# Sliding-window attention with a gated MLP on one core: the order of all steps and the engines of casts and copies, written anew

## The chip, the core and the metric

The kernel runs on one NeuronCore of a Trainium2 chip. TensorE (PE; its weight loads are listed as PEld) multiplies matrices into PSUM, VectorE (DVE), ScalarE (ACT) and GpSimd (POOL) work on elements, SyncE (SP) issues most of the DMAs. The metric is the device time in microseconds; smaller is better. The inputs are q, k and v (float32, 8 batches, 8 heads, 576 positions, 64 values each) and four weights; the output is (8, 576, 512) in float32. Inside, matrices are multiplied in float16.

## What is computed

```python
scores = scale * np.matmul(q, k.transpose(0, 1, 3, 2))
mask = (rel >= 0) & (rel < 64)                 # rel = query position - key position
attn = softmax of scores where mask holds
x = attn @ v, heads side by side               # (8, 576, 512)
h = np.maximum(x @ w_in, 0.0)                  # 1024 columns: u first, then v
u, v = h[..., :512], h[..., 512:]
v_n = (v - mean) / sqrt(var + 1e-6)            # over the 512 columns
v_s = einsum('ts,bsd->btd', w_spatial, v_n) + b_spatial
out = (u * v_s) @ w_out
```

## The kernel before

Each of the 8 batches goes through the same steps. The positions are cut into tiles (indices 0 to 3, and a short one, 4), heads into pairs. A string, ORDER, names 1195 steps one after the other; a loop at its end (L653) splits each word at its dots and calls the function for it. Each engine takes its own instructions in the order in which they come, so this string is the program of all five queues at once; a tile scheduler adds the semaphores but moves nothing. The words, with batch b first:

- `l.b.q.s`, `l.b.k.s` (L301 to L310): loads of q and k by SP. For b below 4 a head pair of 256 KB, and for s = 4 a piece on 64 partitions; from b = 4 on, one head of 144 KB on 32 partitions. `lv.b.n` (L317 to L323): loads of v.
- `c` (L331 to L337): casts of q and k to float16; `cv` (L343, L346): casts of v; `sh` (L351 to L360): a copy of v shifted by 64 partitions. Their last letter is the engine: A ScalarE, D VectorE, P GpSimd.
- `T` (L378, L381): transposes of q and k by PE into PSUM, and `to` (L388, L391), their copies back to SBUF, for b below 4; from b = 4 on `R` (L369) transposes on VectorE.
- `S` (L410, L421): scores by PE; `E` (L453 to L460): the exponential by ScalarE; `M` (L469): the mask as a minimum, by VectorE; `P` (L486, L496): row sums and attention times v by PE; `n1`, `n2` (L502, L509): one over the sum, as logarithm and exponential, by ScalarE; `x` (L517): the product by VectorE, which ends the attention of a tile.
- `wl.half.r` and `wc.half.r` (L251, L254): load and cast of a block of w_in; half 1 is the v half. The loaded blocks share five buffers with the outputs. `wsp` and `wout`: loads by GpSimd's queue; `W`, `wo` (L271, L276): the spatial weight transposed.
- `V.b.j.r0.r1` (L531): the v half of x @ w_in, matmuls r0 to r1 of four; `Q.b` (L543, L546): the short tile of V together with that of O of the batch before; `vo` (L554, L556): relu; `bs` (L562): statistics; `rs` (L569): their root; `ln` (L580): the normalized values.
- `U`, `ru` (L589 to L602): the u half and its relu; `G` (L612), `g` (L619): the spatial matmul and the gate; `O` (L626), `oc` (L633), `st` (L639): output, its eviction and its store by SP.
- `H.n` (L644): n matmuls on a tile of zeros, which keep PE busy in the start.

PSUM buffers: scores and attention outputs share two large ones (tag `att`), so that the third S waits for the first x; all else shares four of one bank each (tag `mm`). An SP load waits for its buffer, and everything behind it on SP's queue waits with it. All loads of SP use eight semaphores in turn, so a ninth waits for the first to land.

Of the kernel before, what the change touches and what calls it, by code (L numbers as in the profile page):

```python
# [14 lines left out]
S = 576  # L15
# [5 lines left out]
keep scratch table l.0.k.0 H.6 id mask l.0.q.1 maskr l.0.q.0 lv.0.1 ones.0 l.0.q.2 ones.1 lv.0.0 H.2  # L21
lv.0.2 c.0.k.0.A l.0.k.1 H.2 l.0.k.2 lv.0.3 T.0.k.0 H.3 c.0.q.0.A l.0.k.3 c.0.q.1.A lv.0.8 T.0.q.0
to.0.q.0.A T.0.q.1 c.0.q.2.D l.0.q.4 to.0.q.1.A small cv.0.0.P to.0.k.0.A sh.0.0.1.D H.4 l.0.k.4
sh.0.0.0.D wl.1.0 c.0.k.1.A S.0.0 E.0.0 T.0.k.1 c.0.k.2.P H.3 lv.0.5 to.0.k.1.D lv.0.4 M.0.0 S.0.1
l.0.q.3 T.0.k.2 cv.0.1.D E.0.1 H.2 wl.1.1 T.0.q.2 sh.0.1.1.P wl.0.1 P.0.0 to.0.k.2.A M.0.1 lv.0.6
n1.0.0 H.3 c.0.k.4.P lv.1.2 n2.0.0 c.0.q.4.P sh.0.1.0.A P.0.1 lv.0.7 c.0.k.3.P n1.0.1 wl.1.3 T.0.k.4
to.0.q.2.A T.0.q.4 l.1.q.0 cv.0.2.D to.0.k.4.A x.0.0 T.0.k.3 n2.0.1 sh.0.2.1.P l.1.k.0 c.0.q.3.A
to.0.q.4.D wc.1.0.P S.0.2 x.0.1 H.4 wl.1.2 cv.0.4.P E.0.2 to.0.k.3.D sh.0.2.0.P wl.0.3 T.0.q.3
wc.1.1.A S.0.4 to.0.q.3.D l.1.q.1 V.0.3.0.1 E.0.4 M.0.2 wl.0.2 S.0.3 wc.0.1.A V.0.2.0.1 E.0.3 lv.1.0
cv.0.3.D P.0.2 V.0.3.1.2 wc.1.3.D wl.0.0 n1.0.2 V.0.0.0.1 sh.0.3.0.D V.0.0.1.2 M.0.3 sh.0.3.1.A  # L30
lv.1.1 n2.0.2 sh.0.4.0.D P.0.3 M.0.4 l.1.k.1 n1.0.3 x.0.2 wc.1.2.P l.1.q.2 P.0.4 n2.0.3 wsp
V.0.3.2.3 n1.0.4 x.0.3 lv.1.3 V.0.0.2.3 V.0.2.1.2 n2.0.4 wc.0.3.A lv.1.4 x.0.4 V.0.3.3.4 V.0.2.2.3
vo.0.3.A V.0.0.3.4 l.1.k.3 wc.0.2.D V.0.2.3.4 c.1.q.0.P vo.0.0.A V.0.1.0.1 l.1.q.3 V.0.1.1.2
vo.0.2.A c.1.k.0.P V.0.1.2.3 wc.0.0.P bs.0.2 Q.0 V.0.1.3.4 T.1.k.0 cv.1.0.P vo.0.1.A U.0.0 vo.0.4.D
c.1.q.1.P to.1.k.0.A bs.0.0 T.1.q.0 U.0.4 c.1.k.1.P to.1.q.0.A bs.0.4 U.0.3 sh.1.0.1.P ru.0.4 lv.1.5
ru.0.0 bs.0.1 S.1.0 ru.0.3 T.1.q.1 U.0.2 E.1.0 bs.0.3 c.1.q.2.P T.1.k.1 sh.1.0.0.A M.1.0 U.0.1
l.1.k.2 to.1.q.1.A l.1.q.4 to.1.k.1.D ru.0.2 W.1 rs.0 l.1.k.4 ru.0.1 W.3 ln.0.4 ln.0.3 W.0 wo.3.A
ln.0.1 P.1.0 wo.1.D cv.1.1.A lv.1.6 ln.0.2 W.4 wo.0.A ln.0.0 l.2.k.0 c.1.k.3.P S.1.1 wo.4.D n1.1.0
W.2 wout lv.1.7 T.1.k.3 wo.2.A T.1.q.2 G.0.1 l.2.k.4 cv.1.2.P to.1.k.3.A l.2.q.0 n2.1.0 sh.1.1.1.P
c.1.k.2.D G.0.0 lv.1.8 to.1.q.2.A c.1.q.3.P sh.1.1.0.A l.2.q.1 g.0.1 E.1.1 T.1.k.2 G.0.4 sh.1.2.1.P  # L40
g.0.0 G.0.2 to.1.k.2.A c.1.k.4.P x.1.0 c.1.q.4.A M.1.1 sh.1.2.0.A S.1.2 g.0.4 T.1.k.4 E.1.2 T.1.q.4
g.0.2 P.1.1 l.2.k.1 T.1.q.3 to.1.k.4.A G.0.3 M.1.2 n1.1.1 lv.2.2 c.2.k.0.D n2.1.1 l.2.k.2 P.1.2
to.1.q.4.D cv.1.3.P g.0.3 n1.1.2 O.0.0 lv.2.1 sh.1.3.1.P x.1.1 n2.1.2 O.0.2 lv.2.0 to.1.q.3.A x.1.2
c.2.q.0.P S.1.3 oc.0.2.D S.1.4 cv.1.4.P E.1.3 T.2.k.0 oc.0.0.D lv.2.3 O.0.3 sh.1.4.0.P to.2.k.0.A
M.1.3 lv.2.5 T.2.q.0 c.2.q.1.P O.0.1 sh.1.3.0.A to.2.q.0.D lv.2.4 E.1.4 P.1.3 oc.0.3.D lv.3.3 n1.1.3
V.1.1.0.2 M.1.4 lv.3.2 V.1.3.0.2 n2.1.3 oc.0.1.D l.2.q.4 V.1.3.2.3 c.2.k.2.A P.1.4 x.1.3 l.2.q.2
cv.2.0.P S.2.0 n1.1.4 V.1.1.2.3 l.2.k.3 n2.1.4 V.1.1.3.4 cv.2.1.P V.1.3.3.4 lv.2.7 x.1.4 vo.1.1.A
U.1.1 c.2.k.1.P vo.1.3.D l.2.q.3 E.2.0 sh.2.1.1.P V.1.2.0.2 sh.2.0.0.D lv.2.6 T.2.q.1 cv.2.2.P
sh.2.0.1.A V.1.2.2.3 bs.1.1 lv.3.6 V.1.2.3.4 ru.1.1 V.1.0.0.2 vo.1.2.A V.1.0.2.3 M.2.0 V.1.0.3.4
c.2.q.4.P T.2.k.1 c.2.k.4.A lv.3.0 P.2.0 to.2.k.1.D vo.1.0.A sh.2.1.0.P st.0.0 Q.1 to.2.q.1.A bs.1.2  # L50
n1.2.0 c.2.k.3.P lv.3.1 bs.1.3 S.2.1 oc.0.4.A sh.2.2.1.P l.4.q.1 U.1.4 vo.1.4.A bs.1.0 lv.3.7
T.2.k.2 cv.3.1.P U.1.3 n2.2.0 l.3.k.0 c.2.q.2.P to.2.k.2.D ru.1.4 E.2.1 U.1.2 cv.2.3.P x.2.0 lv.3.5
c.2.q.3.P bs.1.4 T.2.q.2 ru.1.3 U.1.0 sh.2.2.0.P l.3.q.1 to.2.q.2.A M.2.1 l.3.k.4 rs.1 T.2.k.3
ru.1.2 S.2.2 lv.2.8 ln.1.1 P.2.1 ln.1.0 ru.1.0 l.3.q.0 ln.1.2 n1.2.1 T.2.q.4 ln.1.4 l.3.k.1 T.2.q.3
ln.1.3 G.1.3 to.2.k.3.A l.3.k.3 sh.2.3.1.D to.2.q.3.A to.2.q.4.A G.1.0 st.0.2 E.2.2 st.0.3 n2.2.1
G.1.1 M.2.2 lv.3.4 x.2.1 l.3.q.3 S.2.3 g.1.0 P.2.2 E.2.3 cv.2.4.P l.3.q.2 g.1.3 G.1.4 sh.2.3.0.P
g.1.1 n1.2.2 st.0.1 G.1.2 M.2.3 n2.2.2 l.4.q.2 x.2.2 T.2.k.4 P.2.3 to.2.k.4.A l.3.k.2 c.3.k.3.P
g.1.2 n1.2.3 S.2.4 c.3.k.0.P O.1.1 lv.4.4 g.1.4 E.2.4 c.3.k.4.P l.4.q.7 n2.2.3 O.1.0 sh.2.4.0.P
oc.1.1.D cv.3.0.A l.3.q.4 M.2.4 O.1.2 oc.1.0.A sh.3.0.1.P x.2.3 cv.3.3.A V.2.2.0.4 l.4.k.1 c.3.k.1.P
c.3.q.1.A sh.3.1.0.P oc.1.2.A l.4.k.3 P.2.4 vo.2.2.D O.1.3 n1.2.4 st.0.4 sh.3.0.0.P cv.3.2.D n2.2.4  # L60
sh.3.1.1.P c.3.q.0.A V.2.1.0.4 x.2.4 sh.3.3.1.A oc.1.3.D lv.4.1 c.3.q.2.P V.2.0.0.4 vo.2.1.A bs.2.2
l.4.q.4 c.3.k.2.P T.3.q.0 st.1.3 sh.3.2.1.P vo.2.0.D T.3.k.0 to.3.q.0.A V.2.3.0.4 l.4.k.0 c.3.q.3.P
bs.2.1 to.3.k.0.A T.3.k.2 cv.4.4.P vo.2.3.A T.3.k.1 bs.2.0 S.3.0 sh.3.2.0.P to.3.k.2.A T.3.q.1
lv.4.2 T.3.q.2 to.3.k.1.A c.3.q.4.P to.3.q.1.D l.4.k.2 Q.2 E.3.0 sh.3.3.0.P bs.2.3 S.3.1 vo.2.4.A
M.3.0 T.3.k.3 cv.4.1.P to.3.q.2.A U.2.2 bs.2.4 E.3.1 sh.4.4.0.P P.3.0 to.3.k.3.D ru.2.2 lv.4.0 S.3.2
oc.1.4.D rs.2 lv.3.8 U.2.0 n1.3.0 l.4.q.5 ln.2.2 M.3.1 U.2.1 n2.3.0 E.3.2 l.4.q.6 x.3.0 T.3.q.3
U.2.3 l.4.q.3 ru.2.0 l.4.q.0 M.3.2 to.3.q.3.A P.3.1 st.1.1 ln.2.3 ru.2.1 P.3.2 ln.2.0 lv.4.3 ln.2.1
ru.2.3 T.3.q.4 st.1.2 T.3.k.4 ln.2.4 n1.3.2 G.2.2 to.3.k.4.D st.1.0 to.3.q.4.A l.4.k.5 n1.3.1 G.2.0
# [617 lines left out]
```

## Time and profile before

| what | value |
|---|---|
| median of 5 runs | 213.35 us (212.08 to 216.94) |
| the profiled execution's own time | 215.84 us |
| its span, first to last instruction | 214.1 us |
| mean granted PE clock | 0.99 |
| DMA traffic | 41.47 MB, 194 GB/s over the span |
| short-tile pv matmuls (Q) start at | 28.8, 59.1, 83.2, 106.9, 129.0, 152.3, 173.4 and 194.2 us |

How to read the profile: busy times are those of one execution; "x" is a count of instructions. A row of a group gives line, engine, operation, out<-in and shape, then busy time and the mean of one. In the slices, each digit is the busy share in tenths of 5.35 us. The Q starts cut the run into stages, one per batch: while the gated MLP of one batch runs on PE, the attention of the next is worked in between.

### The profile page before, as it was taken

How to read it: one execution, taken by the hardware profiler on the slowest of the kernel's cores; microseconds unless marked ns; L12 is line 12 of the kernel's file. 1: busy time of each engine (PE TensorE's matmuls, PEld its weight loads, DVE VectorE, ACT ScalarE, POOL GpSimd, SP SyncE). 2: the span in 40 equal slices, each digit the busy share in tenths (PEclk: the TensorE clock that was granted, in tenths of full speed). 3: DMA queues.
4: the chain of work that ended last, by engine and by line, in shares of the span. 5: the costliest groups of instructions: out<-in, count | busy, mean ns of one | idle time of the engine just before them, and what ended most of it. 6: DMA issues, size and time to landing. Idle time of an engine off the chain costs nothing.

```text
span 214.1 us, 6690 instructions
## 1 busy us (share of the span) xinstructions
PE 200.0 (93%) x2726; PEld 106.8 (50%) x2726; DVE 166.8 (78%) x328; ACT 172.4 (81%) x320; POOL 73.7 (34%) x109
## 2 busy tenths in 40 slices
PE   7677899899999999999999998999999999999992
PEld 2344445555555546655555554465554645454450
DVE  2245898799796879979999889888987798778650
ACT  7777979988999699978877799989998798665512
POOL 2126583545761678035300744042303450000000
PEclk9997999999999999999999999999999999999999
DMA  5999999999989999994799799997999423000415
GB/s 179 283 213 298 327 239 240 199 205 227 245 227 228 343 189 239 199 302 62 204 242 184 160 221 234 241 172 214 259 208 174 130 87 126 0 3 21 186 55 182
DMA packets 77742, 41.47 MB, mean 194 GB/s; under 512 B 44368, under 2 KB 72080, under 8 KB 77712
## 3 DMA queue, kind: packets, MB, share of 16 engines
q1 hardware_dynamic: 76544, 39.86, 83.3%
q0 software_dynamic: 1168, 1.19, 3.3%
q8 instruction: 21, 0.34, 0.8%
q14 instruction: 9, 0.07, 0.1%
HBM read 32.79 MB, written 9.44 MB: 197 GB/s over the span
## 4 chain that ended last, share of the span: by engine, by line
PE 58%; ACT 20%; DVE 7%; SPq 4%; issue 4%; DMA 3%; POOL 2%; ACTq 0%; DVEq 0%; POOLq 0%
PE ps L612 17%; PE po L626 9%; PE pu L589 8%; PE pv L531 6%; ACT e L453 4%; PE oz L486 4%; PE sc L421 3%; DMA vf<-in_v_dram 3%; PE oz L496 3%; ACT ln L502 2%; ACT ru L602 2%; ACT zi L509 2%; PE pv L543 2%; ACT vs L556 2%; SPq L301 2%
## 5 line engine op out<-in xcount | busy, mean ns | idle before, releaser
L612 PE MATMUL ps<-wspT,vn 128*128 128x512 f16 (+1 forms) x256 | 38.7, 286 | 0.8 <-DVE wspT L276 0.8
L453 ACT ACTIVATE e<-sc 128x1024 f16<-128x1024 f32 x32 | 32.6, 1026 | 4.8 <-PE sc L410 3.9
L531 PE MATMUL pv<-win,x 128*128 128x512 f16 x128 | 32.2, 382 | 0.9 <-DVE x L517 0.7
L589 PE MATMUL pu<-x,win 128*128 128x512 f16 x128 | 31.4, 379 | 0.0
L619 DVE TENSOR_TENSOR g<-ps,ru 128x512 f16<-128x512 f32 (+1 forms) x40 | 24.6, 629 | 8.2 <-PE ps L612 8.2
L626 PE MATMUL po<-wout,g 128*128 128x512 f16 x128 | 30.8, 380 | 0.0
L517 DVE TENSOR_TENSOR x<-oz,zi 128x512 f16<-128x512 f32 (+1 forms) x40 | 25.1, 630 | 6.3 <-ACT zi L509 5.8
L469 DVE TENSOR_TENSOR e<-e,mask 128x1024 f16<-128x1024 f16 x32 | 26.3, 821 | 4.2 <-ACT e L453 3.9
L502 ACT ACTIVATE ln<-oz 128x512 f32<-128x512 f32 (+1 forms) x40 | 22.0, 554 | 9.1 <-PE oz L496 8.9
L562 DVE BATCH_NORM_STATS2 st<-vs 128x6 f32<-128x512 f16 (+1 forms) x40 | 26.8, 669 | 0.5 <-ACT vs L556 0.4
L612 PEld LDWEIGHTS <-vn 128*128 128x128 f16 x256 | 17.0, 97 | 15.4 <-DVE vn L580 2.1
L509 ACT ACTIVATE zi<-ln 128x512 f32<-128x512 f32 (+1 forms) x40 | 23.4, 594 | 0.7
L602 ACT ACTIVATE ru<-pu 128x512 f32<-128x512 f32 (+1 forms) x40 | 21.1, 553 | 1.4 <-PE pu L594 0.7
L556 ACT ACTIVATE vs<-pv 128x512 f16<-128x512 f32 (+1 forms) x29 | 16.7, 598 | 5.4 <-PE pv L531 3.7
L360 POOL COPY vs<-vn 64x512 f16<-64x512 f16 (+1 forms) x16 | 12.6, 789 | 18.7 <-ACT vn L346 15.0
L633 ACT COPY ob<-po 128x512 f32<-128x512 f32 (+1 forms) x23 | 13.1, 585 | 7.2 <-PE po L626 6.8
L531 PEld LDWEIGHTS <-x 128*128 128x128 f16 x128 | 11.3, 98 | 14.5 <-DVE x L517 2.5
L626 PEld LDWEIGHTS <-g 128*128 128x128 f16 x128 | 11.3, 97 | 12.1 <-DVE g L619 1.1
L589 PEld LDWEIGHTS <-win 128*128 128x128 f16 x128 | 11.6, 98 | 11.5
L612 PE MATMUL ps<-wspT,vlast 65*128 65x512 f16 (+1 forms) x64 | 17.3, 288 | 0.0
L346 POOL CAST vn<-vf 64x512 f16<-64x512 f32 (+1 forms) x12 | 8.1, 683 | 21.7 <-DMA vf<-in_v_dram 21.5
L496 PEld LDWEIGHTS <-vn 128*64 128x64 f16 x320 | 13.6, 112 | 3.2
(130 smaller groups left out, 368.4 us busy)
## 6 DMA issues: line engine op xcount, KB each, us to landing
out_dram<-ob SPq DMA_DIRECT2D x32, 256.0 KB, 3.8
vf<-in_v_dram SPq DMA_DIRECT2D x40, 128.0 KB, 5.8
fq<-in_q_dram SPq DMA_DIRECT2D x32, 144.0 KB, 5.1
fk<-in_k_dram SPq DMA_DIRECT2D x32, 144.0 KB, 5.5
fk<-in_k_dram SPq DMA_DIRECT2D x16, 256.0 KB, 6.2
fq<-in_q_dram SPq DMA_DIRECT2D x16, 256.0 KB, 5.8
vf<-in_v_dram SPq DMA_DIRECT2D x16, 256.0 KB, 5.9
wf<-in_moe_w_in_dram SPq DMA_DIRECT2D x8, 256.0 KB, 5.0
```

The lines of the kernel that those rows point to most:

```text
L453: nc.scalar.activation(e2[:, :, :], sc[0][:, :, :], AF.Exp, bias=0.0, scale=0.125)
L469: nc.vector.tensor_tensor(e2[:, :, :], e2[:, :, :], m, ALU.min)
L502: nc.scalar.activation(lnz[:, 0:n], OZ[b, s][:, 1, 0:n], AF.Ln)
L509: nc.scalar.activation(zinv[:, 0:n], lnz[:, 0:n], AF.Exp, bias=0.0, scale=-1.0)
L517: nc.vector.tensor_tensor(x[:, 0:n], oz[:, 0, 0:n], zinv[:, 0:n], ALU.mult)
L531: nc.tensor.matmul(PV[b, j][0:jn, :], xcol(b, r, j), w_in_sb[:, r, 512:1024], start=(r == 0), stop=(r == 3))
L562: nc.vector.bn_stats(st6[0:jn, 0:6], VSB[b, j][0:jn, :])
L589: nc.tensor.matmul(pu[:, :], w_in_sb[:, r, 128 * m:128 * m + 128], X[b, r][:, :], start=(r == 0), stop=(r == 3))
L602: nc.scalar.activation(RU[b, m][:, 0:n], pu[:, 0:n], AF.Relu)
L612: nc.tensor.matmul(o, VN[b, kk][0:kn, 128 * mm_:128 * mm_ + 128], w, start=(kk == 0), stop=(kk == 4))
L619: nc.vector.tensor_tensor(g[:, :], ps[:, 0:n], RU.pop((b, m))[:, 0:n], ALU.mult)
L626: nc.tensor.matmul(po[:, :], G[b, r][:, 128 * j:128 * j + 128], w_out_sb[:, r, :], start=(r == 0), stop=(r == 3))
```

## The change

ORDER is replaced. Its 1195 steps stay the same set, apart from the engine letters: `c`, `cv`, `sh`, `wc`, `wo`, `to`, `vo` and `oc` steps are spread over the engines in other numbers (A/D/P):

| step | before | after |
|---|---|---|
| casts of q and k (`c`) | 12/7/37 | 13/12/31 |
| casts of v (`cv`) | 11/8/21 | 11/15/14 |
| shifted copies (`sh`) | 14/7/35 | 11/14/31 |
| copies of transposes (`to`) | 28/12/0 | 15/25/0 |
| relu of v (`vo`) | 29/11/0 | 32/8/0 |
| output evictions (`oc`) | 29/11/0 | 27/13/0 |
| w_in casts (`wc`) | 3/2/3 | 3/1/4 |
| spatial weights (`wo`) | 3/2/0 | 2/3/0 |

No function changes. In the start, q is loaded first and k3 third; the v half of w_in comes as blocks 1, 0, 3, 2, the last block of the u half, `wl.0.1`, comes after those of batch 1 have begun; the five groups of H ahead of the first transpose hold 14 matmuls (10 before), and others stand ahead of P.0.0 and after P.0.1. In the last batch U.7.4 and Q.7 come ahead of V.7. Two parts of the diff:

```diff
@@ the start, to U.0.4 @@
-keep scratch table l.0.k.0 H.6 id mask l.0.q.1 maskr l.0.q.0 lv.0.1 ones.0 l.0.q.2 ones.1 lv.0.0 H.2
-lv.0.2 c.0.k.0.A l.0.k.1 H.2 l.0.k.2 lv.0.3 T.0.k.0 H.3 c.0.q.0.A l.0.k.3 c.0.q.1.A lv.0.8 T.0.q.0
-to.0.q.0.A T.0.q.1 c.0.q.2.D l.0.q.4 to.0.q.1.A small cv.0.0.P to.0.k.0.A sh.0.0.1.D H.4 l.0.k.4
-sh.0.0.0.D wl.1.0 c.0.k.1.A S.0.0 E.0.0 T.0.k.1 c.0.k.2.P H.3 lv.0.5 to.0.k.1.D lv.0.4 M.0.0 S.0.1
-l.0.q.3 T.0.k.2 cv.0.1.D E.0.1 H.2 wl.1.1 T.0.q.2 sh.0.1.1.P wl.0.1 P.0.0 to.0.k.2.A M.0.1 lv.0.6
-n1.0.0 H.3 c.0.k.4.P lv.1.2 n2.0.0 c.0.q.4.P sh.0.1.0.A P.0.1 lv.0.7 c.0.k.3.P n1.0.1 wl.1.3 T.0.k.4
-to.0.q.2.A T.0.q.4 l.1.q.0 cv.0.2.D to.0.k.4.A x.0.0 T.0.k.3 n2.0.1 sh.0.2.1.P l.1.k.0 c.0.q.3.A
-to.0.q.4.D wc.1.0.P S.0.2 x.0.1 H.4 wl.1.2 cv.0.4.P E.0.2 to.0.k.3.D sh.0.2.0.P wl.0.3 T.0.q.3
-wc.1.1.A S.0.4 to.0.q.3.D l.1.q.1 V.0.3.0.1 E.0.4 M.0.2 wl.0.2 S.0.3 wc.0.1.A V.0.2.0.1 E.0.3 lv.1.0
-cv.0.3.D P.0.2 V.0.3.1.2 wc.1.3.D wl.0.0 n1.0.2 V.0.0.0.1 sh.0.3.0.D V.0.0.1.2 M.0.3 sh.0.3.1.A
-lv.1.1 n2.0.2 sh.0.4.0.D P.0.3 M.0.4 l.1.k.1 n1.0.3 x.0.2 wc.1.2.P l.1.q.2 P.0.4 n2.0.3 wsp
-V.0.3.2.3 n1.0.4 x.0.3 lv.1.3 V.0.0.2.3 V.0.2.1.2 n2.0.4 wc.0.3.A lv.1.4 x.0.4 V.0.3.3.4 V.0.2.2.3
-vo.0.3.A V.0.0.3.4 l.1.k.3 wc.0.2.D V.0.2.3.4 c.1.q.0.P vo.0.0.A V.0.1.0.1 l.1.q.3 V.0.1.1.2
-vo.0.2.A c.1.k.0.P V.0.1.2.3 wc.0.0.P bs.0.2 Q.0 V.0.1.3.4 T.1.k.0 cv.1.0.P vo.0.1.A U.0.0 vo.0.4.D
-c.1.q.1.P to.1.k.0.A bs.0.0 T.1.q.0 U.0.4 c.1.k.1.P to.1.q.0.A bs.0.4 U.0.3 sh.1.0.1.P ru.0.4 lv.1.5
+id scratch table l.0.q.1 keep H.2 l.0.q.0 mask l.0.k.3 H.3 l.0.k.0 small l.0.k.1 lv.0.0 H.3 lv.0.1
+c.0.q.1.A l.0.q.2 H.4 lv.0.3 c.0.q.0.P lv.0.4 H.2 l.0.k.2 T.0.q.0 T.0.q.1 to.0.q.0.A H.2 wl.1.1
+c.0.k.1.D c.0.k.0.A lv.0.2 to.0.q.1.A T.0.k.0 l.0.q.3 T.0.k.1 maskr to.0.k.0.D H.3 wl.1.0 to.0.k.1.D
+S.0.0 l.0.q.4 c.0.q.2.P cv.0.0.D E.0.0 S.0.1 lv.0.5 c.0.k.3.D E.0.1 sh.0.0.0.D T.0.k.3 l.0.k.4
+T.0.q.2 H.6 to.0.q.2.D sh.0.0.1.A c.0.k.2.P M.0.0 lv.1.0 P.0.0 cv.0.1.D M.0.1 n1.0.0 lv.0.7 T.0.k.2
+sh.0.1.0.A to.0.k.3.D lv.0.6 to.0.k.2.A sh.0.1.1.D P.0.1 c.0.q.3.D n2.0.0 lv.0.8 H.4 n1.0.1 x.0.0
+wl.1.3 n2.0.1 T.0.q.3 wl.1.2 cv.0.2.D S.0.2 c.0.q.4.A l.1.k.1 x.0.1 c.0.k.4.P to.0.q.3.A wl.0.3
+T.0.q.4 sh.0.2.1.D wc.1.1.P E.0.2 l.1.q.0 T.0.k.4 S.0.3 to.0.k.4.D to.0.q.4.D wl.0.2 wc.1.0.A M.0.2
+S.0.4 cv.0.3.P E.0.3 wl.0.0 V.0.3.0.1 V.0.3.1.2 l.1.k.0 sh.0.3.1.D sh.0.2.0.A P.0.2 cv.0.4.D E.0.4
+M.0.3 n1.0.2 V.0.0.0.1 M.0.4 V.0.0.1.2 wc.1.2.P V.0.2.0.1 sh.0.4.0.A V.0.2.1.2 sh.0.3.0.P P.0.3
+n2.0.2 n1.0.3 wc.1.3.P x.0.2 P.0.4 n2.0.3 wsp c.1.k.1.D wl.0.1 V.0.2.2.3 V.0.0.2.3 n1.0.4 lv.1.1
+x.0.3 V.0.3.2.3 n2.0.4 l.1.q.1 c.1.q.0.A wc.0.3.D V.0.3.3.4 lv.1.3 x.0.4 V.0.2.3.4 vo.0.3.A
+V.0.0.3.4 vo.0.2.D l.1.q.2 wc.0.0.A V.0.1.0.1 l.1.k.2 bs.0.3 V.0.1.1.2 vo.0.0.A V.0.1.2.3 l.1.k.3
+V.0.1.3.4 wc.0.2.A wc.0.1.P T.1.q.0 lv.1.2 vo.0.1.A Q.0 to.1.q.0.D c.1.k.0.P U.0.0 l.1.q.3 vo.0.4.A
+cv.1.0.D U.0.4 bs.0.2 ru.0.0 T.1.k.0 U.0.3 sh.1.0.1.D to.1.k.0.A bs.0.4 c.1.q.1.P ones.0 S.1.0
...
@@ the end, from the last batch's pv steps @@
-x.7.2 n1.7.3 O.6.1 oc.6.2.D n2.7.4 n2.7.3 G.6.4 x.7.4 oc.6.1.A x.7.3 V.7.3.0.4 g.6.4 V.7.1.0.4
-V.7.2.0.4 vo.7.1.D vo.7.3.D Q.7 vo.7.2.A bs.7.3 V.7.0.0.4 vo.7.4.A bs.7.2 oc.6.4.A U.7.0 bs.7.4
-vo.7.0.A st.6.4 st.6.1 U.7.4 bs.7.1 U.7.3 ru.7.4 ru.7.0 bs.7.0 U.7.1 rs.7 O.6.3 ru.7.3 ln.7.4 ln.7.0
-U.7.2 ln.7.1 oc.6.3.A ln.7.3 ru.7.1 ln.7.2 st.6.3 G.7.1 ru.7.2 st.6.2 st.6.0 G.7.2 g.7.1 G.7.0 g.7.2
-G.7.3 g.7.0 G.7.4 g.7.3 O.7.0 g.7.4 O.7.1 oc.7.0.A st.7.0 O.7.2 oc.7.1.D st.7.1 O.7.3 oc.7.2.A
-st.7.2 Q.8 oc.7.3.A st.7.3 oc.7.4.A st.7.4
+oc.6.2.D V.7.0.0.4 vo.7.4.D st.6.2 V.7.1.0.4 bs.7.4 oc.6.4.A V.7.3.0.4 vo.7.0.A vo.7.1.D bs.7.0
+V.7.2.0.4 bs.7.1 O.6.3 vo.7.2.A vo.7.3.A bs.7.2 U.7.0 oc.6.3.A bs.7.3 U.7.2 st.6.3 st.6.0 rs.7 U.7.3
+st.6.4 ru.7.0 ln.7.3 U.7.1 ln.7.1 ru.7.3 ln.7.0 ln.7.2 ru.7.2 ln.7.4 G.7.2 ru.7.1 G.7.0 g.7.2 G.7.1
+g.7.0 G.7.3 g.7.1 G.7.4 g.7.3 O.7.0 g.7.4 O.7.1 oc.7.0.A st.7.0 O.7.2 oc.7.1.A st.7.1 O.7.3 oc.7.2.D
+st.7.2 Q.8 oc.7.3.D st.7.3 oc.7.4.A st.7.4
```

## The prediction

> **What bounds the kernel now.** First the page's busy shares and slices, to see where the time isn't filled; columns of the slices run from the start of the span to its end, 5.35 us each.
> ```profile
> PE 200.0 (93%) x2726; PEld 106.8 (50%) x2726; DVE 166.8 (78%) x328; ACT 172.4 (81%) x320; POOL 73.7 (34%) x109
> ...
> PE   7677899899999999999999998999999999999992
> ...
> DVE  2245898799796879979999889888987798778650
> ...
> PEclk9997999999999999999999999999999999999999
> ```
> TensorE is full from slice 5 on. A busy PE can be a waiting one, so the second view, the chain that ended last in order of time, shows at what rate it works (start, length, what):
> ```profile
> 18.76 1.82 PE warm L644 x4
> ...
> 27.14 0.43 DVE x L517
> 27.56 2.65 DVE win L254
> ...
> 114.25 4.44 PE ps L612 x20
> ...
> 200.97 4.93 PE ps L612 x40
> 205.90 3.46 PE po L626 x16
> ```
> Twenty ps matmuls take 4.44 us, 222 ns each, sixteen po 216 ns each: that is the pace of a PE that never waits. Now I add up PE's work after Q.0, the first 64-column pv matmul (28.8 us), at such paces, each from start to next start: V 112 matmuls x 0.216 = 24.2; U 128 x 0.216 and 128 short ones x 0.029 (16 in 0.47) = 31.4; G 160 x 0.222 and 160 short ones x 0.03 = 40.3; O 128 x 0.216 = 27.6; eight Q at 0.88 = 7.0; S, P, T and W by the starts in the timeline (about 0.45, 0.62, 0.25, 0.28 us each, the short P 0.4): 15.8 + 20.2 + 7 + 1.4. Together 175 us. The last matmul starts at 209.96, so 181.2 us were spent. All that a new order could save after Q.0 is about 6 us, and part of it is switching between groups, which no order removes. Before Q.0 PE has 11 to 12 us of work in 28.8 us. So the start is worth most, and the third view was the start by stretches (us; busy of PE, PEld, DVE, ACT, POOL with counts; granted clock; DMA share; GB/s):
> ```profile
> 15.00:20.00 5.00, 3.01 (x44) 1.63 (x45) 2.49 (x5) 3.96 (x8) 3.84 (x7) 0.86 1.08 293
> 20.00:25.00 5.00, 4.76 (x79) 2.65 (x78) 3.67 (x8) 3.87 (x7) 1.34 (x3) 0.80 1.03 332
> 25.00:30.00 5.00, 4.09 (x28) 1.61 (x26) 4.37 (x5) 4.10 (x9) 4.94 (x10) 1.00 1.16 280
> ```
> DMA is saturated (share above 1), the PE clock was at half speed for 3.4 us around 20 us, and at 27.56 a cast of w_in on VectorE lasts 2.65 us in the chain. Three separate things delay Q.0.
>
> **What the change does to the sums.** The steps are the same 1195, the matmuls the same 2726; only order and the engine letters differ. Net by letter: VectorE +11 large and +2 small copies of transposed q and k, +5 casts of q and k, +7 of v, +7 shifted copies, +2 output evictions, -3 v evictions, -1 w_in cast, +1 spatial weight copy. At the rows' means (tr copy 690 ns, small 274, casts about 430, shifted copies about 285, ob 683, vs 686, and 2 x 500 for the wide v copies, between the 285 and 767 that the trace has) that is +13.8 us of VectorE. ScalarE loses 9 us, mostly 13 tr copies, 11 of them at 590; GpSimd loses 9 us (casts and copies at about 610). None of this is on the end's path by itself; the cover is PE, as long as VectorE keeps up.
>
> Where it may not: between Q.0 and Q.1 (28.8 to 59.1 us, 30.3 us long). There the new order gives VectorE 51 steps for 41, 29.2 us for 24.7 by these means; GpSimd 9.8 us for 14.7, ScalarE 26.6 for 30.3. The windows show VectorE busy 25.8 us in 30 to 60. Its instructions overlap by 0.08 us back to back (starts 0.60 apart for 0.69), so the ten extra steps add 4.5 - 0.8 = 3.7 us. Against it stands contention. A cast by VectorE costs 423 ns alone, 2740 at worst:
> ```profile
> L254 POOL CAST win<-wf x3: 610/638/768, 18.5 to 27.6; 128x512 f16<-128x512 f32 x3
> ...
> L254 DVE CAST win<-wf x2: 423/1582/2740, 22.6 to 27.5; 128x512 f16<-128x512 f32 x2
> ```
> The columns are minimum, median and maximum ns, then first and last start. During those 2740 ns GpSimd ran five steps without a pause. The Trainium skill (GPSIMD Engine Reference, 8. Key points) says both things in one list: elementwise work is structurally about twice as fast on VectorE, and the two share their SBUF interfaces, with contention where VectorE runs in a two-port mode. The row agrees with the first only when GpSimd is idle. By the rule's factor alone the 19 SBUF moves would be a gain everywhere; by the row each can cost 0.3 or 2.7 us. I take the middle of the trace: masks (L469) lost 26.3 - 32 x 0.68 = 4.5 us over the run, and the stage after Q.0 holds about 4.4 us of such losses; with GpSimd's work at 9.8/14.7 they fall to 2.9. VectorE then has 25.8 + 3.7 - 1.5 = 28.0 us in 30.3: 92%, where it was 85%. Covered, but barely. In later stages the sums differ by at most 2.3 us in 20 to 24 (21.4 to 23.6, 22.2 to 22.5, 21.6 to 21.9, 21.1 to 22.1, 18.1 to 20.3), with ScalarE and GpSimd no fuller than 25.2 and 13.1; I cost them at nothing, bounds -1 and +2 us.
>
> **The start, step by step.** Landings are DMA records of this trace: 256 KB of q or k every 0.75 to 1.0 us, 128 KB of v every 0.5, the two 64-partition pieces and v's last piece 1.0 each, w_in 0.65. Both orders move the same 6.29 MB up to their seventh w_in block and third batch-1 piece, and this landed at 26.0 us, so I scale the new list to it. It gives q3 at 14.0 (was 18.0), k4 17.4 (15.6), v7 and v6 by 18.9 (21.0), w_in's last block of the v half 21.4 (23.8).
> - Then S.0.2: it waits for a PSUM buffer that x.0.0 frees. Before, VectorE stood 3.5 us for v4 and v5 ahead of x.0.0 (17.61). Now x.0.0 stands before that cast, behind the cast of q3 (14.0 + 0.4) and the chain P, n1, n2, which I put at 15.8; S.0.2 goes from 18.34 to about 16.8.
> - S.0.3: behind k4's cast (18.0) and transpose, 18.4 instead of 21.84. The four warm-up matmuls that held 1.82 us of the chain come earlier, after P.0.1.
> - P.0.3: GpSimd has the w_in cast (21.4 to 22.0) ahead of the shifted copy (22.6): 22.65 instead of 23.92.
> - From P.0.3 to Q.0 it was 4.9 us, of which 1.2 us PE idle before x.0.2 and x.0.3. The new path is P.0.3, n1, n2, x.0.3, the last r = 3 matmuls and V.0.1: 22.65 + 0.7 + 0.6 + 0.65 + 0.7 = 25.3, then 7 matmuls 1.5 us: Q.0 at 26.8, 2.0 us earlier.
> The half clock: the skill (TensorE: Matmul & The Clock Gate, Part 1) has the clock halved after an idle window of about 3.4 us. The row has 0.86 and 0.80 there. If the new order escapes the dip (its S.0.2 comes 1.5 us sooner), PE saves up to 1.7 us that are partly in the 2.0 above; if the dip comes back elsewhere in the start, four warm-ups cost 0.9 us more. I count neither.
>
> A wait is added. The load wl.0.1 now reuses the buffer that wc.1.3, GpSimd's last cast of the first half, frees (about 23.3 us), and it stands on SP's queue ahead of lv.1.1, l.1.q.1 and the rest of batch 1. Next to it GpSimd starts the spatial weights (wsp, 650 KB). Before, a 128 KB load issued at the same moment as wsp (24.53) landed only at 31.89, one issued 0.6 us sooner at 29.77. So wl.0.1 lands between 26.7, in turn, and 30.0, behind wsp; its cast is GpSimd's next, U.0.0 waits for it, and so does GpSimd's cast of l.1.k.0 behind it: U.0.0 at 27.4 to 30.7, where it was 30.16. The nearest row is the load next to wsp, which speaks for the later half; I take 29.0, U.0.0 at 29.7, then half a microsecond of gain; but T.1.q.0 (0.7 us before) was done ahead of Q.0, and batch 1's remaining casts wait less: before, PE lost a further 1.6 us against its own pace between U.0.0 and T.1.q.4 (44.8 us), for transposes whose pieces landed at 34.9 to 40.4; in the new order their cumulated bytes are 1 us ahead of PE's need. Of this I take 1.5 us back. Sum for the likeliest case: 0.5 + 1.5 = 2.0 us.
>
> The tail: last x, V.7, five U and O.6 as cover for the layer norm, G, O, Q.8, one eviction, one store, as before; 4.4 us of U and O stand against about 4.8 us of evictions, statistics and scaling, of which the last is needed 0.9 us later. Nothing, bounds 0 and +0.5.
>
> Against the profiled execution: 215.84 - 2.0 = 213.8 (span 214.1 to 212.1, 1.7 around it). It lies 2.5 us above the median of the runs, 213.35; I carry the difference: 211.4.
>
> **Rivals.** (B) The start's gain is eaten by wl.0.1: it lands at 30 behind wsp, U.0.0 at 30.7, and batch 1 then lies on the same DMA stream as before. DMA's share of 1.03 to 1.24 up to 50 us speaks for it, that PE lagged these landings by 2 us more than needed speaks against. Time 213.3, give or take 1. (C) Slower: between Q.0 and Q.2 VectorE becomes the queue that ends last. Of its ten extra steps several stand in front of a mask, x or g for which PE waits. It decides once VectorE exceeds 95%, 28.8 us in that stage, 0.8 us above my sum. Then each of the ten costs about 0.45 us net of the start's gain: 4.5 - 2.0, 215.8. For it: 25.8 us of 30 already, and a mask that took 2200 ns. Against it: GpSimd has a third less work there, and ScalarE, which carries the chain from 53 to 68 us, has 12% less.
>
> **Numbers.** Likeliest (A), 211.4, own range 209 to 212.3: 0.45. B: 0.24. C: 0.31. The range 208.8 to 216.3 takes A's lower bound (all of the 2 us and the clock dip) and C's centre with 0.5. What a measurement can tell from no change is 0.5%, 1.07 us. Faster 0.44, within 0.24, slower 0.32.
>
> **What would show it.** Right: the first 64-column pv at or below 27.3 us, the first pu by 29.9, PE from Q.0 to its last matmul at or below 181.5, VectorE 27 to 28.5 us busy in the stage. Wrong: pu later than 30.2 with POOL waiting for wf (B); x and g ahead of PE's waits, VectorE above 9.5 in 10 between 40 and 80 us (C). A new stretch at half clock after 22 us, or stores holding loads on SP longer than the 17.8 us seen, would break the sum from outside.

## The result and the profile after

| | before | after |
|---|---|---|
| median | 214.10 us (74 runs, 212.08 to 218.41) | 213.08 us (39 runs, 211.96 to 214.63) |
| the profiled execution's own time, span | 215.84, 214.1 us | 213.94, 212.2 us |
| first Q (64-column pv) | 28.78 us | 28.59 us |
| last matmul starts | 209.96 us | 208.02 us |

The ratio of after to before is 0.9964 [0.9949, 0.9979]: 0.36% less time, 0.8 us. That is faster, but by less than the 0.5% that one measurement of this kernel can tell from no change. The forecast was 211.4 us, 0.9% less than the 213.35 it started from. The direction was right, the size was not. Runs that were disturbed are left out of ratios, which is why a ratio can differ from the quotient of two medians.

The page of the changed kernel, busy shares and slices (5.3 us each):
```profile
PE 198.9 (94%) x2726; PEld 106.8 (50%) x2726; DVE 173.8 (82%) x359; ACT 163.7 (77%) x305; POOL 64.9 (31%) x93
...
PE   7677799899999999999999999998999999999992
...
DVE  2586698999899988876999989979999689969642
...
PEclk9999799999999999999999999999999999999999
```
VectorE is 7.0 us busier, not 13.8. Of the 6.8 us between, 2.9 lie in the 32 masks (L469), which now last 730 ns on average, 821 before; the rest was not followed up. ScalarE loses 8.7 us (9 forecast), GpSimd 8.8 (9 forecast). PE is as full as before, from slice 6 on (the first slice counted as 1).

The start by stretches, with the same columns as the lines shown for before:
```profile
15.00:20.00 5.00, 3.68 (x78) 2.26 (x78) 3.84 (x9) 4.97 (x9) 1.27 (x2) 1.00 1.29 191
20.00:25.00 5.00, 4.48 (x53) 2.28 (x52) 2.72 (x6) 3.50 (x7) 2.79 (x5) 0.66 1.04 346
25.00:30.00 5.00, 3.91 (x20) 1.57 (x19) 4.03 (x9) 4.94 (x11) 3.45 (x6) 1.00 1.08 250
```
The stretch at half clock has not gone. It moved: 15 to 20 us runs at full clock and does 78 matmuls where it did 44, then the clock falls to 0.66 in 20 to 25 us.

The chain that ended last, in this kernel (a piece begins where the one ahead of it ends, so its start can lie 0.1 us behind that of the instruction), from the last block of the v half of w_in to U.0.0 and on to the first spatial matmul:
```profile
16.90 5.86 DMA wf<-in_moe_w_in_dram
...
22.81 0.71 POOL win L254
23.53 0.57 POOL vs L358
...
24.14 0.48 PE oz L496 x12
...
25.93 0.70 DVE x L517
...
26.68 1.76 PE pv L531 x7
...
28.66 0.98 PE pv L543 x4
29.64 0.97 PE pu L589 x4
...
31.95 0.62 ACT vlast L245
...
35.38 0.31 ACT lnv L569
...
39.11 1.84 PE ps L612 x25
```
A w_in block lands at 22.76; GpSimd casts it at once (win); behind it on the same queue stands the shifted copy of v (vs L358), whose own input had been there since 21.34; half of P.0.3 (oz) waits for that copy until 24.14. PE itself stands still for only 0.15 us there, because the half clock has held it up as well; Experiment 3 takes the two apart.

### The profile page after: what moved, and what is told of

Its sections match the earlier page's. It is cut to its first block, busy times and chain, and to the rows that moved or that the text cites. A ratio compares the mean times of both kernels' runs of the same rounds, so it can differ in the third digit from the quotient of the medians.

```text
span 212.2 us, 6682 instructions
## 1 busy us (share of the span) xinstructions
PE 198.9 (94%) x2726; PEld 106.8 (50%) x2726; DVE 173.8 (82%) x359; ACT 163.7 (77%) x305; POOL 64.9 (31%) x93
## 4 chain that ended last, share of the span: by engine, by line
PE 62%; DVE 11%; ACT 8%; SPq 7%; DMA 5%; POOL 3%; issue 1%; POOLq 0%
PE ps L612 14%; PE po L626 10%; PE pv L531 10%; PE pu L589 9%; SPq L317 4%; PE sc L421 3%; PE oz L486 3%; PE oz L496 3%; DMA wf<-in_moe_w_in_dram 3%; PE pv L543 3%; DVE st L562 3%; DMA out_dram<-ob 2%; SPq L301 2%; ACT e L453 2%; PE pu L594 2%; ACT ru L602 2%
## 5 line engine op out<-in xcount | busy, mean ns | idle before, releaser
L589 PE MATMUL pu<-x,win 128*128 128x512 f16 x128 | 30.5, 380 | 0.1
L619 DVE TENSOR_TENSOR g<-ps,ru 128x512 f16<-128x512 f32 (+1 forms) x40 | 24.1, 627 | 3.6 <-PE ps L612 2.3
L469 DVE TENSOR_TENSOR e<-e,mask 128x1024 f16<-128x1024 f16 x32 | 23.4, 730 | 3.1 <-ACT e L453 2.9
L556 ACT ACTIVATE vs<-pv 128x512 f16<-128x512 f32 (+1 forms) x32 | 18.6, 598 | 6.5 <-PE pv L531 6.3
L633 ACT COPY ob<-po 128x512 f32<-128x512 f32 (+1 forms) x21 | 12.1, 587 | 8.7 <-PE po L626 6.5
L496 PE MATMUL oz<-e,vn 128*64 128x64 f16 x320 | 14.3, 197 | 0.0
```

The source lines that it names most:

```text
L469: nc.vector.tensor_tensor(e2[:, :, :], e2[:, :, :], m, ALU.min)
L496: nc.tensor.matmul(oz[64 * h:64 * h + 64, 0, c0:c0 + 64], vt, e2[:, h, c0:c0 + 64], start=True, stop=True)
L589: nc.tensor.matmul(pu[:, :], w_in_sb[:, r, 128 * m:128 * m + 128], X[b, r][:, :], start=(r == 0), stop=(r == 3))
L619: nc.vector.tensor_tensor(g[:, :], ps[:, 0:n], RU.pop((b, m))[:, 0:n], ALU.mult)
```

## Where in the run the time went

One measure goes through all experiments. For each step on PE take its start minus the work of all PE steps ahead of it in the order, at the paces of the prediction (matmuls on zeros count as no work): this **lag** grows when PE waits or is slowed. Its level at Q.0 is what the start costs; what is added later is lost later. From the matmul starts of each profiled execution, in us:

| profiled execution | at Q.0 | Q.0 to Q.1 | Q.1 to Q.4 | Q.4 to Q.8 | at Q.8 |
|---|---|---|---|---|---|
| before, the first | 17.50 | +0.79 | +0.48 | +1.48 | 20.25 |
| before, again | 16.79 | -0.24 | +0.84 | +1.76 | 19.15 |
| after, the first | 16.83 | +0.69 | -0.34 | +1.13 | 18.31 |
| after, again | 16.88 | +0.69 | -1.20 | +1.26 | 17.63 |
| old start, new rest | 17.46 | +0.51 | -1.47 | +1.13 | 17.63 |
| the same, again | 15.81 | +0.28 | -0.77 | +1.25 | 16.57 |
| old up to Q.1, new rest | 17.62 | -0.02 | -0.98 | +0.27 | 16.89 |

Two things stand out. The start of the kernel before is 0.7 us better in its second execution than in the one that the prediction was built on, and level with the new start. And the new rest, behind either start, gives 0.3 to 1.5 us back between Q.1 and Q.4 where the old one loses 0.5 to 0.8: the gain lies in stages that the prediction had costed at nothing.

The theory after the result was therefore: the start is no gain, the later stages are. The rival: the start is the gain, as forecast, and later stages lose part of it. A second rival was that the engine letters alone do it.

## Experiment 1: start and rest apart, each twice

`head_new` has the new order and letters up to and with Q.0 and what is left of the old; `head_old` the reverse. All is computed.

```diff
 head_new (against before)
-keep scratch table l.0.k.0 H.6 id mask ... wc.0.0.P bs.0.2 Q.0
+id scratch table l.0.q.1 keep H.2 l.0.q.0 ... lv.1.2 vo.0.1.A Q.0
...
 head_old (against before)
 keep scratch table ... bs.0.2 Q.0
-V.0.1.3.4 T.1.k.0 cv.1.0.P vo.0.1.A U.0.0 vo.0.4.D
+c.1.k.1.D l.1.k.2 bs.0.3 V.0.1.3.4 T.1.q.0 vo.0.1.A to.1.q.0.D U.0.0 vo.0.4.A
...
```

> The new order and letters up to Q.0, then every remaining step in the old order with the old letters. Theory 1, the start: the new kernel's gain over the old one (about 0.8 us of 214) is made before Q.0, where its PE is 0.7 us ahead for the same work, and the rest of the order is neutral: ratio to the kernel before 0.996 to 0.997, first short pv matmul at about 28.6 us. Theory 2, the stages: the gain comes after Q.0, from ScalarE work moved to VectorE, and a start that is ahead only waits longer at the first G: ratio 0.999 to 1.001.

> The old order and letters up to Q.0, then every remaining step as in the new kernel. Theory 1: ratio to the kernel before 0.999 to 1.001, because the start is the old one. Theory 2: 0.996 to 0.997, and the profile loses less than the old one between Q.3 and the end (about 1 us there).

Measured: `head_new` 214.74 us, 1.0034 [1.0003, 1.0065]; `head_old` 212.18 us, 0.9908 [0.9869, 0.9948]. The new start alone makes the old kernel slower, and the old start makes the new kernel faster. So that this doesn't hang on one comparison, all four were run again on another chip:

> The kernel before, unchanged, as one more entrant: ratio 1.000, its interval is what this comparison can tell. Its second profile shows which of the differences between the first profiles (1.9 us of span, while the medians differ by 0.8) belong to the order and which to one execution. If the loss of 0.7 us at U.4.1 and at G.6.2 is in the order, it is there again.

> The new kernel, unchanged. By its own runs 0.995 to 0.998. By theory 2' (the new order is worth about 1.5 to 2 us after Q.0, and its start costs about 1 us, as head_old and head_new suggest) the same; by theory 1 (start ahead, stages neutral), which the two hybrids speak against, also: this run is the measure for the other two of this call. Its second profile shows whether the 1.2 us that its first lost against head_old between O.1.1 and Q.3, with the same code there, was one execution's.

> The old start up to Q.0 and the new order behind it, once more, on the same chip as the new kernel. Theory 2' (new stages gain, new start loses): 0.988 to 0.994, clearly below the new kernel of this call. If the first figure was chance: as the new kernel, 0.995 to 0.998.

> The new start up to Q.0 and the old order behind it, once more. Theory 2': 1.001 to 1.006. If the profiles tell the start rightly (0.7 to 0.9 us ahead at Q.0): 0.995 to 0.998.

Measured, in this order: 214.60 us, 1.0015 [0.9983, 1.0046]; 213.15, 0.9936 [0.9903, 0.9968]; 212.12, 0.9898 [0.9838, 0.9958]; 215.38, 1.0038 [1.0007, 1.0068]. Both signs repeat. The rest of the new order is worth about 1.0%; the new start costs 0.2 to 0.4% ahead of the old rest (0.2 where the kernel before itself stands at 1.0015) and 0.4 to 0.6% ahead of the new one. The costs of the start are small beside their intervals, whose lower ends only just clear 1; that it brings no gain is what the four runs show. The rival "the start is the gain" has fallen.

Why the prediction saw a gain in the start: it measured against an execution in which the old start was unusually late. In before's second execution no slice of the start is at half clock, and the cast of w_in on VectorE that took 2740 ns, beside five steps of GpSimd, and stood in the chain takes 427, with no cast or copy of GpSimd beside it (casts by L254 there: minimum, median, maximum ns; then a stretch):
```profile
L254 DVE CAST win<-wf x2: 427/427/427, 22.4 to 26.8; 128x512 f16<-128x512 f32 x2
...
20.00:25.00 5.00, 3.69 (x85) 2.21 (x83) 4.02 (x9) 4.95 (x9) 0.70 (x2) 1.00 1.01 331
```

## Experiment 2: letters without order, order without letters

`letters_new` is the old order with the new engine letters (143 of 1195 words differ), `letters_old` the new order with the old letters.

```diff
 letters_new (against before), one stretch
-vo.2.0.D T.3.k.0 to.3.q.0.A V.2.3.0.4 l.4.k.0 c.3.q.3.P bs.2.1 to.3.k.0.A T.3.k.2 cv.4.4.P
+vo.2.0.A T.3.k.0 to.3.q.0.A V.2.3.0.4 l.4.k.0 c.3.q.3.P bs.2.1 to.3.k.0.D T.3.k.2 cv.4.4.D
...
 letters_old (against after), one stretch
-vo.2.1.D sh.3.1.1.A cv.3.0.P l.4.q.1 lv.4.1 to.3.k.0.D O.1.3 sh.3.1.0.A
+vo.2.1.A sh.3.1.1.P cv.3.0.A l.4.q.1 lv.4.1 to.3.k.0.A O.1.3 sh.3.1.0.P
```

> The old order of steps, with the engine letters of the new one. Theory 1: the letters don't shorten the start, since loads and PE order there are the old ones; more steps on VectorE behind the same loads cost 0 to 1.5 us: ratio 1.000 to 1.007. Theory 2: the relief of ScalarE is what counts, ratio 0.996 to 0.998. If VectorE at over 90% is a danger at all, as the prediction's slower case had it, it shows here: over 1.007.

> The new order of steps with the old engine letters: the counterpart of the run that was 3.7% slower. Theory 4: order and letters are fitted to each other, neither carries the gain alone: 1.005 to 1.03. Rival: the order carries the gain, and the letters (more VectorE) are what costs: 0.985 to 0.995.

Measured: `letters_new` 222.22 us, 1.0369 [1.0310, 1.0428]; `letters_old` 224.53 us, 1.0470 [1.0426, 1.0515]. Neither half of the change does anything by itself but harm: order and letters fit each other, and either one with the other's partner costs six to thirteen times what the pair gains. Where `letters_new` loses most (PE waits 3.2 us for copies of transposes, its longest wait), from its chain (start, length, what):
```profile
80.82 0.69 DVE vs L554
81.51 0.61 DVE st L562
...
82.33 0.37 DVE nk L331
82.69 0.61 DVE st L562
...
83.42 0.66 DVE tr L388
84.08 0.33 DVE vn L346
84.41 0.61 DVE st L562
...
85.23 1.18 DVE tr L388 x2
...
86.45 0.42 PE sc L410 x14
```
Each of these instructions of VectorE starts as the one ahead of it ends (80.82 + 0.69 = 81.51), and PE's scores wait for three copies of transposes (tr) which stand among statistics (st), casts (nk, vn) and an eviction (vs) that these scores don't need. This is rival C's mechanism, but not by its measure. Over the whole run VectorE is 80% busy here, less than the 82% of the faster kernel after: what counts here is what stands ahead of the awaited instruction in the queue, not the queue's share. In `letters_old` VectorE is busy 74%, and PE's waits are spread (the longest, 2.4 us, is for a cast of k on ScalarE); all six of its executions also have a mean clock of 0.992 or less, so part of its 4.7% is the clock, and its cause is not taken apart.

## Experiment 3: two moved steps that the prediction had not priced

In the chain of after, two steps stand ahead of awaited work: the w_in cast ahead of the shifted copy on GpSimd, and `ones.0` (vlast L245, a fill of one row) on ScalarE. The new order moved `ones.0` and `ones.1` from the idle start into the first layer norm. The row of L245 in before, then in after (the start times are the last figures before the shape):
```profile
L245 ACT ACTIVATE vlast<-scratch x2: 608/616/625, 3.5 to 4.0; 1x512 f16<-1x512 f16 x2
```
```profile
L245 ACT ACTIVATE vlast<-scratch x2: 625/626/626, 32.0 to 39.6; 1x512 f16<-1x512 f16 x2
```
`copy_first` takes the copy ahead of the cast, `ones_early` takes both fills to the front, `ones_copy` does both.

```diff
 copy_first (against after)
-V.0.0.1.2 wc.1.2.P V.0.2.0.1 sh.0.4.0.A V.0.2.1.2 sh.0.3.0.P P.0.3
+V.0.0.1.2 sh.0.3.0.P wc.1.2.P V.0.2.0.1 sh.0.4.0.A V.0.2.1.2 P.0.3
...
 ones_early (against after)
-l.0.q.1 keep H.2
+l.0.q.1 keep ones.0 ones.1 H.2
...
-ones.0 S.1.0
+S.1.0
...
-ones.1 to.1.q.2.D
+to.1.q.2.D
```

> The new kernel with one step moved: GpSimd's shifted copy for head pair 3 of batch 0 (sh.0.3.0.P) stands ahead of its cast of the w_in block 2 (wc.1.2.P), which waits for its load until 22.76 us; in the new kernel's profile the copy is done at 24.09 only, and P.0.3 waits for it. Theory 1a, this queue holds the start: P.0.3 ends about 2 us sooner, n1, n2, x.0.3 and Q.0 by 1.0 to 1.5 us, ratio to the kernel before 0.990 to 0.993 (2.0 us less than before at most). Rival 1b, the w_in blocks or the half clock at 21 to 24 us hold it: Q.0 by less than 0.4 us, ratio 0.995 to 0.997 as the new kernel.

> The new kernel with its two one-row fills (ones.0, ones.1, 0.62 us of ScalarE each) put back to the head of ScalarE's queue, where it is idle. In the new kernel's first profile the first of them lies in the chain that ended last (31.95 us), ahead of the reluctant path relu, statistics, root, layer norm, first G. Theory 3: that step is most of what the new start costs after Q.0 (its PE falls 1.2 us further behind from U.0.0 to T.1.q.4, the old one's 0.4 in an undisturbed execution): first G of batch 0 0.4 to 0.6 us earlier against PE's work, ratio to the kernel before 0.990 to 0.993 where the new kernel has 0.994 to 0.996. Rival: the layer norm waits for VectorE's queue (three spatial copies in it), ones is hidden: ratio unchanged.

> Both moved steps in the new kernel: ones early, and the shifted copy ahead of the w_in cast. If they add up: 0.988 to 0.992. If the start's end is set by one thing behind the other, as ones_early.

Measured: `copy_first` 212.77 us, 0.9939 [0.9908, 0.9970]; `ones_early` 212.75, 0.9933 [0.9902, 0.9965]; `ones_copy` 212.29, 0.9899 [0.9847, 0.9951]. Each stands beside 0.9964 and 0.9936 of the new kernel itself: a single move is not told apart from nothing. Both together are lowest, with an interval that still touches the new kernel's.

The profiled executions say more of the start. All of these have the new start; n1 is the first step on ScalarE behind P.0.3:

| profiled execution | half clock between 20 and 25 us | copy behind the cast | n1 of P.0.3 starts | Q.0 starts |
|---|---|---|---|---|
| after, twice | yes | yes | 24.64, 24.77 | 28.59, 28.64 |
| `head_new`, twice | no | yes | 24.47, 24.47 | 28.35, 28.35 |
| `copy_first` | yes | no | 24.60 | 28.48 |
| `ones_copy` | no | no | 22.82 | 26.70 |

Either one alone holds P.0.3 to 24.5 or 24.6 us; only in the execution with neither does Q.0 come at the 26.8 of the prediction. (`ones_early` has the copy behind the cast and no half clock up to 25 us: n1 at 24.48. So the fills are not what makes the difference. Its half clock came behind 26 us, and Q.0 at 29.99.) The four V matmuls ahead of P.0.3, and the wait within it, in after and then in `head_new`:
```profile
21.42 1.89 PE L531 MATMUL pv<-win,x 128*128 128x512 f16 x4
...
24.14 0.27 PE L496 MATMUL oz<-e,vs 128*64 128x64 f16 x2 [0.15 <-POOL vs L358]
```
```profile
21.66 1.04 PE L531 MATMUL pv<-win,x 128*128 128x512 f16 x4
...
24.05 0.22 PE L496 MATMUL oz<-e,vs 128*64 128x64 f16 x2 [0.90 <-POOL vs L358]
```
In the brackets is PE's idle time and what ended it. That an earlier Q.0 reaches the end is not shown: the seven executions of `copy_first` with a mean clock of at least 0.996, which by this table should have it, have a median of 212.87 us, no better than the rest of them.

From Q.0 to G.0.1 the lag grows 1.42 us in `ones_copy`, where it grew 1.50 in after: the fill was in the chain, but taking it out frees little, since ScalarE's next exponential and three relus are due at that point anyway.

## Experiment 4: matmuls on zeros against the half clock

If the half clock follows idle PE time, six more matmuls on zeros after P.0.1 in the kernel before should prevent it.

```diff
-sh.0.1.0.A P.0.1 lv.0.7
+sh.0.1.0.A P.0.1 H.6 lv.0.7
```

> The kernel before with six more matmuls on zeros after P.0.1, where PE waits for pieces of k and q (15.7 to 17.5 us). In two of three executions of the old start with a profile the clock was halved near 19 us, and PE was 0.7 to 1.7 us later at Q.0 than in the others. Theory 5: the half clock needs a window in which PE does little; filled, it doesn't come, and the kernel gains what the halved executions lose on average: 0.2 to 0.8 us, ratio 0.996 to 0.999, no PE clock below 0.95 in 15 to 25 us. Rival: the extra matmuls only delay the transposes: 1.000 to 1.003.

Measured: 216.12 us, 1.0043 [1.0001, 1.0084], although the profiled execution, with no slice at half clock, took 213.43, the lowest of the twelve. Seven of its twelve executions have a mean clock of at least 0.996, and their median is still 215.38: the clock was full and the time lost nevertheless. In the same comparison 10 of 23 executions of the kernel before have that clock too, so it isn't shown that the six matmuls hold it. PE executed 1.3 us more work (six at about 0.22) ahead of the scores that come next; whether that is all of it stays open.

## Experiment 5: which of the later stages

`late_cut` keeps the old order up to and with Q.1; `mid_new` has the old start, the new order from Q.0 to Q.4, and then the old again.

```diff
 late_cut (against before), after Q.1
-to.2.q.1.A bs.1.2 n1.2.0 c.2.k.3.P lv.3.1
+st.0.2 lv.2.8 bs.1.3 st.0.1 to.2.q.1.D n1.2.0 bs.1.0 c.2.q.2.P
...
 mid_new (against before), after Q.4
-vo.4.3.A c.5.q.1.P l.6.q.1 bs.4.0
+st.3.0 lv.6.0 l.6.q.4 st.3.2 sh.6.4.0.P l.6.k.5 l.6.q.2 l.6.k.7 l.6.k.3 vo.4.0.A bs.4.0
```

> The old order and letters up to and with Q.1, then the new order's rest; all is computed. Start kept old followed by the new rest from Q.0 took 0.990 of the kernel before. Theory 1, the new order gains after Q.1, where the traces of before lose PE time at U.4.1 and G.6.2: 0.990 to 0.993 again, lag of PE from Q.1 to the end at most 0.8 us (1.96 and 2.6 in the two traces of before). Rival 1, it gains in batch 0's gated MLP, Q.0 to Q.1: 0.998 to 1.002. Rival 2, the two orders don't fit at a seam and any seam costs: over 1.003.

> The old order up to Q.0, the new from there to Q.4, the old after it; all is computed. Theory 1, split evenly by the two places in the traces (U.4.1 ahead of Q.5 and G.6.2 after it): about half the gain of the new rest, 0.994 to 0.997. Rival 1, all the gain lies ahead of Q.4: 0.989 to 0.992. Rival 2, all lies after Q.4, where U.4.1 and G.6.2 are: 0.998 to 1.002. Rival 3, a seam costs: over 1.003.

Measured: `late_cut` 212.84 us, 0.9950 [0.9909, 0.9991], lag from Q.1 to the end -0.71 us (before: +1.96 and +2.60). `mid_new` 215.75 us, 1.0054 [1.0005, 1.0102]. `late_cut` says that there is a gain after Q.1 without the new first stage, though its interval ends just under 1; its ratio is above the expected 0.990 to 0.993, which its interval still takes in. `mid_new` goes the way of "a seam costs". Up to Q.4 its lag falls by 1.0 us, as in the other kernels with the new middle; then it rises by 3.8 us between G.4.2 and O.4.1. Its chain there, and the stretches:
```profile
127.56 1.73 SPq L310
...
131.93 6.33 DMA vf<-in_v_dram
...
138.29 0.43 DVE vn L346
138.71 0.60 DVE e L469
```
```profile
135.00:140.00 5.00, 3.06 (x72) 1.57 (x65) 2.09 (x5) 2.69 (x6) 0.00 (x0) 1.00 1.21 225
140.00:145.00 5.00, 4.70 (x72) 2.74 (x66) 4.01 (x9) 3.51 (x7) 2.37 (x3) 0.67 0.73 182
```
At the seam loads that the old order issues from 123.9 us on stand one behind the other on SP's queue, with stores between them; a piece of v issued at 131.93 lands at 138.26, its cast stands on VectorE, and masks and gates behind it wait. In before the same piece landed little sooner, at 137.10 (issued at 130.87), but PE came to its work 3.3 us later (Q.4 at 129.03, here at 125.77): the new middle runs ahead of the loads of the old rest. PE idles 1.9 of 5 us, and a stretch at 0.67 of the clock follows. So `mid_new` measures its seam and leaves open how the gain divides at Q.4; the three single places in the traces (each named by the step at its end) are:

- O.2.0 to S.4.0: +0.7 and +1.1 us in the two executions of before. Of the six with the new middle four have 0.1, the others 0.5 and 0.8.
- U.4.1: +0.7 and +1.0 in before, none in any kernel with the new order ahead of it, `mid_new` among them.
- G.6.2: +0.8 in both of before and in `mid_new`, which is old there; 0.1 in after.

The new order has one such place of its own, S.6.0: +1.0 us in after, behind a cast of q (nq) on VectorE of 1.63 us; with `late_cut` the lag rises 0.15 there. What one of these losses looks like, from the chain of before ahead of U.4.1:
```profile
123.16 0.90 ACT vs L358
...
124.57 0.98 ACT vs L360
...
127.60 1.83 ACT e L453 x2
...
129.46 1.34 DVE e L469
```
Two shifted copies of v and an eviction stand on ScalarE ahead of the exponentials that P.5.0 and P.5.1 need, and the mask of P.5.0 behind them lasts 1.34 us.

## Why the prediction missed

**The sum came out on the profile and not on the median.** For the profiled execution the forecast was 213.8 us and 213.94 was measured. That agreement is luck, of errors with opposite signs: by the lag, after gained 0.7 us on this execution up to Q.0 and 0.1 us from there to Q.1, where 2.0 us had been forecast, and 1.2 us behind Q.1, where nothing had been. So it is with U.0.0: forecast at 29.7, it came at 29.6, but with Q.0 1.8 us later than forecast and `wl.0.1` landing 1.3 us sooner; in before's second execution U.0.0 is at 29.5, and nothing is gained.

**Failed step 1: "It lies 2.5 us above the median of the runs, 213.35; I carry the difference".** This is what made 211.4 of 213.8. Of the 1.7 us by which 211.4 was too low, 0.75 is the base: the median of five runs was that much below the one of 74. The rest is the gain, 2.0 us forecast and 0.8 to 1.0 measured. The profiled execution was late in just the stretch that the gain was worked out from: a half clock of 3.4 us and a cast of 2740 ns, neither of which is there in the second execution. A gain computed against that stretch contains part of the disturbance, and most executions don't have that part to give back.

**Failed step 2: Q.0 "2.0 us earlier".** It came at 28.59 in place of 28.78. S.0.2 (16.70, forecast 16.8) and S.0.3 (18.44, forecast 18.4) were right to 0.1 us. P.0.3 was not, for two reasons that ran side by side. "W_in's last block of the v half 21.4" landed at 22.76 (at 22.05 to 22.54 in `ones_copy`, `copy_first` and `head_new`), and GpSimd's copy, whose place behind that cast the prediction had seen, was done at 24.09 and not at 22.6. And the half clock, which the prediction had named and not counted, came from about 21.0 to 24.4 us: four V matmuls took 1.89 us in place of 1.04, so that P.0.3 began at 23.24 only. Its second half began at 24.14, in place of 22.65. The table of Experiment 3 shows that each alone is enough. The list of loads as a whole runs 0.9 us late by then (l.1.k.0 landed at 26.97, not 26.04; v7 and v6, "by 18.9", at 20.05 and 20.61); why is not shown.

**Failed step 3: "Of this I take 1.5 us back".** From U.0.0 to T.1.q.4 the lag grew 1.2 us in after, 1.4 and 0.3 in before. The prediction put that loss on landings of batch 1; the chain has the first layer norm there (ScalarE's relus and exponentials, then vn on VectorE up to 39.07), which the change doesn't shorten.

**Failed step 4: later stages "at nothing, bounds -1 and +2 us".** Sums of busy time by engine did not differ, so no price was given. The gain is there: about 1.0% by `head_old` (0.9908 and 0.9898), so 2 us, 1 us beyond the bound on that side; `late_cut`, from Q.1 on, has 1.1 us with an interval of 0.2 to 1.9, so that the bound itself was too narrow rests on `head_old`. Busy sums can't show the gain: what was looked at of the old order's losses (U.4.1 above) is awaited instructions that stand behind others.

**What held.** Rival B did not occur: `wl.0.1`, issued at 23.56, landed at 27.70 and not at 30, as `wsp` was issued only at 24.83; U.0.0 came from Q.0. From Q.0 to the last matmul PE took 179.4 us, under the 181.5 that were named as a sign of being right, but by the later stages that had been put at nothing. VectorE's load in the stage was right, 28.0 forecast and 27.74 measured over 30 to 60 us. Rival C didn't decide this kernel. Between 40 and 80 us VectorE stood at 9.3 to 9.4 of 10, under the 9.5 that was named, and PE waited for it once, 0.3 us for an x. One reading was off without consequence: the cast rows, 423 ns on VectorE and 610 on GpSimd, are 1.4 times apart, and so agree only roughly with "about twice". The stage, and one stretch of it:
```profile
30.00:60.00 30.00, 29.22 (x411) 17.12 (x410) 27.74 (x59) 26.42 (x48) 11.72 (x19) 1.00 1.10 229
60.00:70.00 10.00, 9.95 (x134) 5.48 (x132) 9.37 (x22) 9.87 (x20) 1.83 (x3) 1.00 0.92 261
```
PE misses 0.05 us of 10 with VectorE at 9.37 of 10.

**Still open.** How the 2 us of the later stages divide between Q.1 to Q.4 and after Q.4 was not settled; single executions differ by 1 us at a place. Why the new start costs 0.2 to 0.6% is known in part: without a half clock the old start has Q.0 at 28.07, 27.09 and 27.12 us (before again, `head_old` again, `mid_new`), the new one, held by its copy, at 28.35; with one, the old has 28.73 to 28.90 and the new 28.59 and 28.64. So at Q.0 the old start is about 0.7 us or more better off without a half clock, the new one 0.3. How much of that reaches the end, and what the two fills add, these single executions can't say. `head_old` (212.1 to 212.2) and `ones_copy` (212.3) beat both kernels. The old start, with the new rest, is what the runs support.

## What to carry to other kernels

Before a gain is worked out of one profiled execution, ask which of its stretches are peculiar to that execution (a half clock, one instruction at several times its own minimum), and price against the minimum; a gain on a disturbed stretch is not carried to the median. In a kernel whose queues are written out by hand, busy sums by engine are no guide at this scale (here they showed neither the gain of 1% nor the losses of 4%): go along each awaited instruction and list what stands ahead of it on its engine, in all stages and not only the one with idle time. Where two waits run side by side, as the copy and the half clock did, taking one away shows nothing; only an execution without both tells what they cost. And engine letters and order belong together, so a test of one without the other measures the misfit.

## What the runs showed of the chip

The half clock comes and goes from execution to execution of the same program. In after, 0.66 over 5 us is 3.4 us at half speed. Half speed over 3.4 of 213 us takes 0.008 off the mean granted clock of a run, which sorts all runs of the two kernels on all chips, those beside the experiments too (the number of stretches is inferred from the clock):

| mean clock | before: runs, median us | new: runs, median us |
|---|---|---|
| 0.996 and above (none) | 41, 213.79 | 22, 212.66 |
| 0.987 to 0.995 (one) | 59, 214.43 | 29, 213.19 |
| below (two or more) | 16, 215.97 | 0 |

One stretch goes with 0.5 to 0.6 us more, two with 2.2. Between runs with none, the new kernel is 1.1 us (0.5%) ahead; and it had no run of 51 with two, before 16 of 116. In mid-run one came behind 5 us in which PE idled for 1.9 (`mid_new`, above), so it is no matter of the start alone. What sets it off is not shown. In the 8 us ahead of it PE's longest pause between matmuls was 0.80 us in before and 0.55 in after; without any half clock, before's second execution has the same 0.80 there and `head_new` 0.55. An idle window of 3.4 us, as the prediction had it, stands ahead of neither, nor of the one in `mid_new`.
